# A fused attention and MLP kernel: PSUM banks placed by its planner, head halves of the second token chunk, ReLU over two column blocks, last output in two pieces

## Chip, cores and metric

The kernel runs on one core of a Trainium2 chip. The metric is the device time of one execution in microseconds (us), as the median of several runs. All times below are in us.

## What is computed

There are two stages. The first is attention with a window of 128 tokens and 4 sink tokens; the second is a layer norm and a two-layer MLP with a residual. Batch is 4, heads 8, sequence 768, head size 64, so the model width is 512 and the hidden width 2048.

```python
scores = scale * np.matmul(q, k.transpose(0, 1, 3, 2))
keep = is_sink | in_window            # pos < 4, or 0 <= i - j < 128
a = softmax(np.where(keep, scores, -1e9))
x = np.matmul(a, v)                   # then heads side by side: (4, 768, 512)
xn = (x - mu) / np.sqrt(var + 1e-6) * g_ln
out = x + np.maximum(xn @ w_ch1, 0.0) @ w_ch2
```

Inputs and output are float32; the matrix products run in bfloat16.

## The kernel before

**Tiles.** The 3072 tokens are 24 tiles of 128, six to a batch (tile t is batch t // 6, place r = t % 6). The MLP works on groups of tiles, `GROUPS = [2, 2, 2, 4, 4, 4, 4, 2]`; groups 0 to 2 are batch 0.

**Order.** Nothing is issued in program order. Each piece of work is an `Op` with a cost by engine, a list of ops it needs, the buffers it allocates and uses, and a key. `Plan.emit` (L56) is a list scheduler: it keeps a clock for each engine, finds when each waiting op could start, takes the engine with the earliest start and, among the ops within a small slack of that start, the one with the lowest key; then it emits its instructions. So the order on each engine is fixed at build time by the planner's costs, and on the chip each engine follows it and waits where its inputs are late. Until 26 us of the planned time, `spin` (L194) fills TensorE's planned gaps with matmuls on a constant tile.

**PSUM.** Of the eight banks, four form two wide buffers of two banks (`ps_w`: scores, values, the sinks' v product, batch 1's q/k transposes), one is the bank for transposes of normalized tiles and for the spins (`ps_t`, "bank"), and three are single (`ps_m`: batch 0's q/k transposes, up and down projections, sink scores). Buffers of a pool are handed out in turn.

**Loads.** POOL issues the loads of q, k, v and both weights in one order (`load`, with at most seven in flight in the plan). Batch 0's q and k come in two token chunks of 384: chunk 0 in two halves of four heads for each of q and k, chunk 1 in one piece for q and one for k (L314). The two v tiles of the first rows come before chunk 1. Then come w1 and w2 by quarters (L351, L354) with v tiles between them, and batch 1's q and k as one piece each (L314). Batches 2 and 3 are loaded by tile (L329) and transposed by DMA from SP's queue (`prep`, L411).

**Attention.** Batches 0 and 1 are transposed on TensorE (`prep_runs`, L388) and copied out of PSUM by ACT (L184) or DVE (L186). `scores` (L500) multiplies a tile's keys with 256 queries; for tiles 0 to 3 the mask is added by a matmul (L496). ACT takes the exponential (L511); for other tiles DVE (L515, L521) or POOL (L523, L526) masks it. `sinks` multiplies the four sink keys (L436, L459, L464) and builds the sinks' values (L446, L451). `values` (L560, L567, L570) multiplies with v; DVE then divides (L592, L594), takes statistics (L600, L603) and centers with the gain `gb` (L608). `gb` is spread over the partitions once by a matmul (L737) and copied by ACT or DVE. Tiles below 12 are transposed on TensorE (L647), later ones by DMA from SP (L637).

**MLP.** `up` (L668) makes one 128-column block of the hidden layer for a group: four matmuls of 128 x n tokens, where n is 256 for groups of two tiles and 512 for groups of four. ReLU (L677 on ACT, L679 on DVE) copies it to SBUF. `down` (L699) multiplies a tile with w2 in four quarters of four matmuls with 512 columns, and DVE adds the residual (L712); SP stores the tile (L717).

The few lines of the planner and of `up` that the change rests on:

```python
if len(h) + k >= b.bufs:                      # Plan.emit.ready
    for u in h[k - b.bufs].users:
        if u.end is not None:
            r = max(r, u.end)
...
pb.t = ps_m.tile([128, 512], FP32, name="pm") # up
for j in range(NDM):
    nc.tensor.matmul(pb.t[:, 0:n], lhsT=w1s[:, j, 128 * ht:128 * (ht + 1)], rhs=xtb[g].t[:, j, 0:n], ...)
```

Of the kernel before, what the change touches and what calls it, by code (L numbers as in the profile page):

```python
# [14 lines left out]
class Buf:  # L15


    def __init__(self, pool, bufs):
        self.pool, self.bufs, self.users, self.t = pool, bufs, [], None
# [12 lines left out]
class Plan:  # L32
# [12 lines left out]
    EARLY = 16.0  # L45

# [9 lines left out]
    def emit(self):  # L56
        free, hist = {}, {}
        waiting = list(self.ops)

        def ready(o):  # L60

            r, held = 0.0, False
            for d in o.deps:
                if d.end is None:
                    return None, False

                r = max(r, d.end - (self.LAT[d.eng] + d.lat - 0.03 if len(o.engs) == 1 and d.eng in o.engs else 0.0))
            n = {}
            for b in o.alloc:
                h = hist.get(b.pool, [])  # L70
                k = n[b.pool] = n.get(b.pool, -1) + 1
                if len(h) + k >= b.bufs:
                    for u in h[k - b.bufs].users:
                        if u.end is not None:
                            r = max(r, u.end)
                        elif b.pool == "pw":
                            held = True
                        else:
                            return None, False
            return (None if held else r), held  # L80

        trace = []
        while waiting:
# [22 lines left out]
            if e == "PE" and s < self.WARM:  # L106
                f = max(free.get(e, 0.0), 1.3)
                n = int((min(s, 5.0) - f) / 0.107) if f < 5.0 else 0
                n += int((s - max(f, 5.0) - 0.1) / 0.057) if s > 5.0 else 0
                for _ in range(n if s < 7.0 else 4 * n // 5):  # L110
                    self.spin()
            free[e] = s + c
            o.end, o.eng = s + c + self.LAT[e] + o.lat, e
            for b in o.alloc:
                hist.setdefault(b.pool, []).append(b)
            waiting.remove(o)
# [7 lines left out]
def kernel(  # L124
# [31 lines left out]
    NB0 = 3  # L156
# [18 lines left out]
    ps_w = ctx.enter_context(tc.tile_pool(name="ps_w", bufs=2, space=PS))  # L175
    ps_t = ctx.enter_context(tc.tile_pool(name="ps_t", bufs=1, space=PS))
    ps_m = ctx.enter_context(tc.tile_pool(name="ps_m", bufs=3, space=PS))
# [11 lines left out]
    bank = ps_t.tile([128, 512], FP32, name="bank")  # L189
    pt_view, junk = bank[:, 0:384].bitcast(BF16), bank[:, 384:512]  # L190
    ident = consts.tile([128, 128], BF16)

    def spin():
        nc.tensor.matmul(junk, lhsT=spinner, rhs=spinner, start=True, stop=True, skip_group_check=True)  # L194
# [81 lines left out]
    ident_done = op({"POOL": 0.35}, const_ident, [begun], -499.5)  # L276
    half_masks = op({"POOL": 0.6}, const_masks, [begun], -492)
# [90 lines left out]
    def prep_runs(b, c, hp, key):  # L368
# [5 lines left out]
        kb, pb = kqb[b], Buf("pm", 3) if n > 1 else Buf("pw", 2)  # L374

        def go(_):
            if kb.t is None:
                kb.t = qkt.tile([128, 2, HP, S], BF16, name="qkt")
            if n > 1:
                pb.t = ps_m.tile([128, 512], FP32, name="pm").bitcast(BF16)[:, 0:2 * w]  # L380
            else:
                pb.t = ps_w.tile([128, 2, 512], FP32, name="pw").rearrange("d x m -> d (x m)").bitcast(BF16)
            pb.t = pb.t.rearrange("d (x m) -> d x m", x=2)
            for x in range(2):
                src = qn[(b, x)].t.rearrange("p (c h r d) -> p c h r d", c=n, h=H, r=e)
                for r in range(e):
                    for h2 in range(2):
                        nc.tensor.transpose(pb.t[64 * h2:64 * (h2 + 1), x, 128 * r:128 * (r + 1)],  # L388
                                            src[:, c, 2 * hp + h2, r, :], ident)
# [3 lines left out]
        for xs in ([(0, 1)] if n > 1 else [(0,), (1,)]):  # L393
            def back(eng, x0=xs[0], x1=xs[-1] + 1):
                copy(eng, kb.t[:, x0:x1, hp, c * w:(c + 1) * w].rearrange("d x (p r) -> d x p r", r=e),
                     pb.t[:, x0:x1, 0:w].rearrange("d x (r p) -> d x p r", r=e))

            m = len(xs) * w
            o = op({"DVE": 0.18 + m * 0.00101, "ACT": 0.16 + m * 0.00084}, back, [o0], key, (), [pb, kb])
            for x in xs:  # L400
                prepped[(b, c, hp, x)] = o
# [26 lines left out]
    def sinks(b, key):  # L428
# [3 lines left out]
        pb, eb = Buf("pm", 3), Buf("es", 2)  # L432
# [8 lines left out]
        vb = Buf("pw", 2)  # L441

        def mm_v(_):
            vb.t = ps_w.tile([128, 2, 512], FP32, name="pw")
            for half in range(2):
                nc.tensor.matmul(vb.t[:, half, 0:4 * (D + 1)], lhsT=sel,  # L446
# [3 lines left out]
        def mul_v(_):  # L450
            nc.vector.tensor_tensor(  # L451
                vs.rearrange("p (a h) d -> p a h d", a=2),
                vb.t[:, :, 0:4 * (D + 1)].rearrange("p a (h d) -> p a h d", d=D + 1),
                smask.rearrange("p (a h) -> p a h", a=2).unsqueeze(3).to_broadcast([128, 2, 4, D + 1]), op=ALU.mult)

        def mm(_):
            pb.t = ps_m.tile([128, 512], FP32, name="pm")
# [9 lines left out]
        ov = op({"PE": 0.22}, mm_v, [vcast[(b, 0)], sinks_done, ones_done], key, [vb])  # L467
        vs_done[b] = op({"DVE": 0.7}, mul_v, [ov, vread.get((b - 2, RB - 1))], key, (), [vb])
# [5 lines left out]
    def scores(t, halves, key):  # L474
# [7 lines left out]
        pbs, ebs = [Buf("pw", 2) for _ in parts], [Buf("e", 8) for _ in parts]  # L482
# [6 lines left out]
        def mm(_):  # L489
            for pb, eb, part in zip(pbs, ebs, parts):  # L490
                eb.t = epool.tile([128, 2, 512 // n, n], BF16, name="e")
                pb.t = ps_w.tile([128, 2, 512], FP32, name="pw").rearrange("p a (i c) -> p a i c", c=n)
# [53 lines left out]
    def values(t, key):  # L546
# [3 lines left out]
        pb = Buf("pw", 2)  # L550
# [3 lines left out]
        def mm(_):  # L554
            po = pb.t = ps_w.tile([128, 2, 512], FP32, name="pw")
# [85 lines left out]
        pt = Buf("pt", 1)  # L641

        def tr(_):
            room()
            pt.t = pt_view
# [14 lines left out]
    def up(g, ht, key):  # L660
        n = 128 * GROUPS[g]
        pb = Buf("pm", 3)
        hb = h1b[(g, ht)] = Buf("h1t", NH1 + 6) if n == 512 else Buf("h1n", NB0 * NH1)

        def mm(_):
            pb.t = ps_m.tile([128, 512], FP32, name="pm")
            for j in range(NDM):
                nc.tensor.matmul(pb.t[:, 0:n], lhsT=w1s[:, j, 128 * ht:128 * (ht + 1)], rhs=xtb[g].t[:, j, 0:n],  # L668
                                 start=(j == 0), stop=(j == NDM - 1))

        def act(e):
            if n == 512:
                hb.t = h1pool.tile([128, 512], BF16, name="h1t", bufs=NH1 + 6)
            else:
                hb.t = h1pool.tile([128, 256], BF16, name="h1n", bufs=NB0 * NH1)
            if e == "ACT":
                nc.scalar.activation(hb.t[:, 0:n], pb.t[:, 0:n], AF.Relu)  # L677
            else:
                nc.vector.tensor_scalar_max(hb.t[:, 0:n], pb.t[:, 0:n], 0.0)  # L679

        deps = [turned[FIRST[g] + i] for i in range(GROUPS[g])] + [w_in[(1, ht // 4)]]
        o = op({"PE": 0.865 * n / 512}, mm, deps, key, [pb], [xtb[g]])
        relu[(g, ht)] = op({"ACT": 0.16 + 0.44 * n / 512, "DVE": 0.15 + 0.54 * n / 512}, act, [o], key - 20, [hb], [pb])
# [3 lines left out]
    def down(g, ti, quarter, key):  # L687
        t = FIRST[g] + ti
        alloc = []
        if quarter == 0:  # L690
            pcb[(g, ti)] = Buf("pm", 3)
            alloc = [pcb[(g, ti)]]
        pb = pcb[(g, ti)]

        def mm(_):
            if quarter == 0:
                pb.t = ps_m.tile([128, 512], FP32, name="pm")
            for ht in range(4 * quarter, 4 * quarter + 4):
                nc.tensor.matmul(pb.t, lhsT=h1b[(g, ht)].t[:, 128 * ti:128 * (ti + 1)], rhs=w2s[:, ht, :],  # L699
# [3 lines left out]
        o = op({"PE": 0.865}, mm, [relu[(g, ht)] for ht in hts] + [w_in[(2, max(quarter, 2))], pre_down.get((g, ti))], key,  # L703
               alloc, [pb] + [h1b[(g, ht)] for ht in hts])
        pre_down[(g, ti)] = o
        if quarter == 3:
# [3 lines left out]
            def fin(_):  # L710
                ob.t = opool.tile([128, DM], FP32, name="ot")
                nc.vector.scalar_tensor_tensor(ob.t, in0=pb.t, scalar=rsb[g][:, ti:ti + 1],  # L712
                                               in1=xb[t].t.rearrange("p h d -> p (h d)"),
                                               op0=ALU.mult, op1=ALU.add)

            def put(_):
                nc.sync.dma_start(out[b, 128 * r:128 * (r + 1), :], ob.t)  # L717

            o = op({"DVE": 0.75}, fin, [o, rs_done[g]], key - 20, [ob], [pb, xb[t]])
# [13 lines left out]
    gp = Buf("pm", 3)  # L733

    def spread_g(_):
        gp.t = ps_m.tile([128, 512], FP32, name="pm")
# [3 lines left out]
    gb_done = op({"ACT": 0.6, "DVE": 0.65}, lambda e: copy(e, gb, gp.t), [gb_done], bkey[0] - 1, (), [gp])  # L740

    for half in range(2):
        for x in range(2):
            load_runs(0, 0, x, 4 * half, 4 * half + 4, ((1.5, 1.0), (1.6, 1.1))[half][x], -500 + half)
    for r in range(2):
        load_v(0, r, -491 + r)
    for x in range(2):
        load_runs(0, 1, x, 0, H, (2.8, 2.04)[x], -488 + x)
# [11 lines left out]
    for b in range(B):  # L760
        k0 = bkey[b]
        if b == 0:
            for c in range(2):
                for hp in range(HP):
                    prep_runs(0, c, hp, k0 + (0.6 + 0.1 * hp if c else 0.15 if hp > 1 else -40))
# [31 lines left out]
    for s, g in mlp_order:  # L797
        if s == "u" and g < NB0:
            for ht in range(NH1):
                up(g, ht, 5.2 * (ht // 4) + 1.73 * g + 0.43 * (ht % 4))  # L800
        elif s == "u":
            for ht in range(NH1):
                up(g, ht, up_pos[g] + 0.216 * GROUPS[g] * ht)
        else:
            order = [(ti, qu) for ti in range(GROUPS[g]) for qu in range(4)]
            for n, (ti, qu) in enumerate(order):
                down(g, ti, qu, down_pos[g] + 0.865 * n)
# [38 lines left out]
```

## Time and profile before

| | |
|---|---|
| median of 4 runs | 235.71 (234.17, 234.78, 236.63, 237.29) |
| the profiled execution | 234.17, span 232.5 from first to last instruction |
| mean granted TensorE clock | 0.998 |
| TensorE busy | 221.8 (95%), 1838 matmuls |
| VectorE, ScalarE, GpSimd busy | 114.8, 115.4, 78.4 |
| loaded from and stored to HBM | 27.27 MB, 6.29 MB |

PE is TensorE's matmuls, PEld its weight loads, DVE is VectorE, ACT ScalarE, POOL GpSimd; SP only issues DMAs. A matmul's recorded duration holds the way through the array: neighbours overlap, and what one costs is the distance between two starts. In the timeline and the chain a row gives start, length, engine, line and the tiles written and read, and a bracket gives the idle time before it and what ended it.

### The profile page before, as it was taken

The page shows a single profiled execution, that of the slowest core. Times are in us where ns is not written, and L with a number is a line of the kernel's source. Part 1 is how long each engine was busy: PE and PEld are TensorE (multiplying, and loading weights), DVE is VectorE, ACT ScalarE, POOL GpSimd, SP SyncE. Part 2 cuts the span into 40 slices and gives each one's busy share as a digit, 9 for nine tenths or more (in the row PEclk, how much of TensorE's full clock was granted, in tenths as well). Part 3 has the DMA queues.
Part 4 walks back from the last instruction along what each step waited for, and adds up shares of the span by engine and source line. Part 5 has one row for each costly group of instructions (what it writes and reads, how often), then busy time and mean ns, then how long its engine had stood idle before and what let it go on. Part 6 is the DMA issues. An engine that isn't in the chain of part 4 may idle for free.

```text
span 232.5 us, 4451 instructions
## 1 busy us (share of the span) xinstructions
PE 221.8 (95%) x1838; PEld 124.3 (53%) x1838; DVE 114.8 (49%) x213; ACT 115.4 (50%) x186; POOL 78.4 (34%) x105
## 2 busy tenths in 40 slices
PE   8977999989899999999999999999999999999993
PEld 8643678867455554454555444454444554445851
DVE  1454676066959698755567345662017560022011
ACT  2658787879451625675314873336623156400810
POOL 7985386459121997191201100210005020000000
PEclk9999999999999999999999999999999999999999
DMA  6999999999997999999952202212002221012102
GB/s 69 147 187 193 191 207 204 205 157 155 140 129 183 136 166 179 142 166 142 154 160 68 25 0 71 71 50 62 0 4 81 77 73 20 0 45 93 45 0 90
DMA packets 83478, 24.93 MB, mean 107 GB/s; under 512 B 74241, under 2 KB 80385, under 8 KB 83458
## 3 DMA queue, kind: packets, MB, share of 16 engines
q0 software_dynamic: 60416, 13.64, 68.6%
q1 hardware_dynamic: 23040, 11.02, 24.0%
q8 instruction: 14, 0.23, 0.4%
q14 instruction: 6, 0.05, 0.1%
q10 hardware_dynamic: 2, 0.00, 0.0%
HBM read 27.27 MB, written 6.29 MB: 144 GB/s over the span
## 4 chain that ended last, share of the span: by engine, by line
PE 83%; DVE 7%; DMA 3%; POOL 3%; ACT 2%; issue 1%; POOLq 0%
PE pm L699 36%; PE pm L668 32%; PE pw L500 4%; DMA qkn<-in_k_dram 3%; PE pw L567 2%; PE pw L570 2%; POOL qkn L314 2%; DVE xn L608 1%; PE pw L560 1%; ACT qkt L184 1%; PE bank L647 1%; DVE st L600 1%; DVE xt L594 1%; DVE qkt L186 1%; POOL vn L338 1%; PE pw L388 1%
## 5 line engine op out<-in xcount | busy, mean ns | idle before, releaser
L668 PE MATMUL pm<-xnt,w1s 128*128 128x256 bf16 (+1 forms) x512 | 88.6, 326 | 0.1
L668 PEld LDWEIGHTS <-w1s 128*128 128x128 bf16 x512 | 48.3, 98 | 33.3 <-issue 2.4
L511 ACT ACTIVATE e<-pw 128x1024 bf16<-128x1024 f32 x44 | 43.5, 1021 | 44.2 <-PE pw L500 44.2
L699 PE MATMUL pm<-w2s,h1t 128*128 128x512 bf16 x256 | 57.9, 379 | 0.0
L712 DVE SCALAR_TENSOR_TENSOR ot<-pm,rs,xt 128x512 f32<-128x512 f32 x24 | 18.0, 749 | 61.1 <-PE pm L699 45.8
L677 ACT ACTIVATE h1t<-pm 128x512 bf16<-128x512 f32 x59 | 35.2, 597 | 21.7 <-PE pm L668 21.7
L699 PEld LDWEIGHTS <-h1t 128*128 128x128 bf16 x256 | 24.2, 98 | 28.4 <-issue 0.8
L699 PE MATMUL pm<-w2s,h1n 128*128 128x512 bf16 x128 | 30.0, 379 | 0.0
L677 ACT ACTIVATE h1n<-pm 128x256 bf16<-128x256 f32 x56 | 21.0, 386 | 17.5 <-PE pm L668 15.2
L620 POOL TENSOR_SCALAR ve<-mv 128x2 f32<-128x2 f32 (+1 forms) x8 | 4.8, 601 | 56.4 <-DVE mv L603 56.3
L338 POOL DMA_DIRECT2D vn<-in_v_dram x24 | 21.6, 916 | 0.4 <-DMA qkn<-in_k_dram 0.4
L523 POOL TENSOR_SCALAR_AFFINE_SELECT e<-e 128x512 bf16<-128x512 bf16 (+1 forms) x7 | 4.9, 700 | 44.3 <-ACT e L511 44.3
L608 DVE SCALAR_TENSOR_TENSOR xn<-xt,mv,gb 128x512 bf16<-128x512 bf16 x24 | 18.5, 774 | 2.3 <-DMA xnt<-xn 1.6
L521 DVE TENSOR_TENSOR e<-e,mask 128x1024 bf16<-128x1024 bf16 x23 | 16.3, 710 | 4.9 <-ACT e L511 4.8
L699 PEld LDWEIGHTS <-h1n 128*128 128x128 bf16 x128 | 11.6, 98 | 12.8 <-issue 0.8
L600 DVE BATCH_NORM_STATS2 st<-xt 128x6 f32<-128x512 bf16 x24 | 16.7, 695 | 0.8
L594 DVE TENSOR_TENSOR xt<-pw,rc 128x512 bf16<-128x512 f32 x24 | 16.6, 692 | 0.8
L567 PE MATMUL pw<-vn,e 128*128 128x65 bf16 x192 | 15.8, 193 | 0.0
L567 PEld LDWEIGHTS <-e 128*128 128x128 bf16 x192 | 13.6, 97 | 2.4 <-issue 0.5
L500 PE MATMUL pw<-qkt 64*128 64x256 bf16 (+1 forms) x192 | 14.7, 263 | 0.1
L570 PE MATMUL pw<-vn,e 128*128 128x65 bf16 x160 | 14.2, 193 | 0.0
L500 PEld LDWEIGHTS <-qkt 64*128 64x128 bf16 x192 | 6.7, 94 | 11.2 <-issue 10.5
(62 smaller groups left out, 171.7 us busy)
## 6 DMA issues: line engine op xcount, KB each, us to landing
out_dram<-ot SPq DMA_DIRECT2D x24, 256.0 KB, 2.2
vn<-in_v_dram POOLq DMA_DIRECT2D x24, 128.0 KB, 10.2
w1s<-in_moe_w_ch_dram POOLq DMA_DIRECT2D x4, 512.0 KB, 12.2
w2s<-in_moe_w_ch_dram POOLq DMA_DIRECT2D x4, 512.0 KB, 14.7
qkn<-in_q_dram POOLq DMA_DIRECT2D x12, 128.0 KB, 7.3
qkn<-in_k_dram POOLq DMA_DIRECT2D x12, 128.0 KB, 7.0
qkn<-in_q_dram POOLq DMA_DIRECT2D x1, 768.0 KB, 18.2
qkn<-in_k_dram POOLq DMA_DIRECT2D x1, 768.0 KB, 19.8
```

Of the source, the lines that this page charges most:

```text
L338: nc.gpsimd.dma_start(vn_buf[b % 2][:, r, :, 0:D], v[b, :, 128 * r:128 * (r + 1), :].rearrange("h p d -> p h d"))
L500: nc.tensor.matmul(pb.t[:, h2, i], lhsT=kb.t[64 * h2:64 * (h2 + 1), 1, hp, 128 * r:128 * (r + 1)], rhs=kb.t[64 * h2:64 * (h2 + 1), 0, hp, ...
L511: nc.scalar.activation(eb.t, pb.t, AF.Exp, scale=scale)
L567: nc.tensor.matmul(pv[:, half, hh, :], lhsT=weights_of(t, half, i, h2, 0), rhs=vn[:, r, h, 0:D + 1], start=fresh and hh == 0, stop=(r == 0 ...
L570: nc.tensor.matmul(pv[:, half, hh, :], lhsT=weights_of(t - 1, half, i, h2, 128), rhs=vn[:, r - 1, h, 0:D + 1], start=False, stop=True, ski ...
L594: nc.vector.tensor_tensor(xb[t].t.rearrange("p (a h) d -> p a h d", a=2), pv[:, :, :, 0:D], rc[0].unsqueeze(3).to_broadcast([128, 2, 4, D] ...
L600: nc.vector.bn_stats(st, xf)
L608: nc.vector.scalar_tensor_tensor(xnb[t].t, in0=xf, scalar=mvb[g][:, ti, 0:1], in1=gb, op0=ALU.subtract, op1=ALU.mult)
L668: nc.tensor.matmul(pb.t[:, 0:n], lhsT=w1s[:, j, 128 * ht:128 * (ht + 1)], rhs=xtb[g].t[:, j, 0:n], start=(j == 0), stop=(j == NDM - 1))
L677: nc.scalar.activation(hb.t[:, 0:n], pb.t[:, 0:n], AF.Relu)
L699: nc.tensor.matmul(pb.t, lhsT=h1b[(g, ht)].t[:, 128 * ti:128 * (ti + 1)], rhs=w2s[:, ht, :], start=(ht == 0), stop=(ht == NH1 - 1))
L712: nc.vector.scalar_tensor_tensor(ob.t, in0=pb.t, scalar=rsb[g][:, ti:ti + 1], in1=xb[t].t.rearrange("p h d -> p (h d)"), op0=ALU.mult, op1 ...
```

## The change

1. *Banks.* There is one PSUM pool with fixed buffers: two wide ones (banks 0 to 3) and four single ones (banks 4 to 7). The planner itself picks the buffer that comes free first (`place`, in `emit`); an op may only be planned when the buffer's last user has been planned. The fourth single buffer, the former transposes bank, serves only spins until a planned time of 26 and joins the others then; spins end when it has been taken. Transposes of normalized tiles take a single buffer.
2. *Order in the first 22 us of the plan.* Among ops that start less than 0.5 after the chosen one, and before it would nearly be done, one with a lower key goes first (`HOLD`).
3. *Loads.* Chunk 1 of batch 0's q and k comes in two halves of four heads. The first half is issued before the first two v tiles, the second half after them. The constant for transposes and the masks are made after all four loads of chunk 0.
4. *Copies.* Chunk 0's first two head pairs are copied out of PSUM as q and k apart, instead of both at once; its other two pairs are copied by DVE only. `gb` is copied by DVE only.
5. *Sinks' values.* Batch 0 takes two single buffers for them instead of a wide one; the product on DVE is two instructions instead of one.
6. *ReLU.* For groups of two tiles, `up` fills one bank with two column blocks (eight matmuls) and one ReLU instruction covers both.
7. *Last output.* For the last tile, `down` runs the four quarters for columns 0 to 383, adds the residual and stores them, and then does the same for columns 384 to 511.

```diff
+    HOLD = 22.0, 0.5
...
+        def place(o):
+            r, taken, now = 0.0, [], free.get("PE", 0.0)
+            for b in o.alloc:
+                if b.pool not in ("pw", "pm"):
+                    continue
+                best = None
+                for i in ((0, 2) if b.pool == "pw" else (4, 5, 6) if now < self.WARM else (4, 5, 6, 7)):
+                    v = vacant(i)
+                    if i not in taken and v is not None and (best is None or v < best[0]):
+                        best = v, i
+                if best is None:
+                    return None, b.pool == "pw"
+                r, b.slot = max(r, best[0]), best[1]
+                taken.append(b.slot)
+            return r, False
...
-            if e == "PE" and s < self.WARM:
+            if s < self.HOLD[0]:
+                s, e, o, c = min((x for x in cand if x[1] == e0 and (x[2] is o or x[2].key < o.key - 0.05 and
+                                  x[0] < min(s + c - 0.12, s + self.HOLD[1]))), key=lambda x: (x[2].key, x[0]))
+            if e == "PE" and s < self.WARM and 7 not in tenant:
...
-    ps_w = ctx.enter_context(tc.tile_pool(name="ps_w", bufs=2, space=PS))
-    ps_t = ctx.enter_context(tc.tile_pool(name="ps_t", bufs=1, space=PS))
-    ps_m = ctx.enter_context(tc.tile_pool(name="ps_m", bufs=3, space=PS))
+    psum = ctx.enter_context(tc.tile_pool(name="psum", bufs=1, space=PS))
...
+    wide = [psum.tile([128, 2, 512], FP32, name=f"wide{i}") for i in range(2)]
+    single = [psum.tile([128, 512], FP32, name=f"single{i}") for i in range(4)]
...
-    ident_done = op({"POOL": 0.35}, const_ident, [begun], -499.5)
-    half_masks = op({"POOL": 0.6}, const_masks, [begun], -492)
+    ident_done = op({"POOL": 0.35}, const_ident, [begun], -498.5)
+    half_masks = op({"POOL": 0.6}, const_masks, [begun], -498)
...
-        for xs in ([(0, 1)] if n > 1 else [(0,), (1,)]):
+        for xs in ([(0, 1)] if c or n > 1 and hp > 1 else [(0,), (1,)]):
...
+            if n > 1 and c == 0 and hp > 1:
+                del engs["ACT"]
...
-        vb = Buf("pw", 2)
+        vb = [Buf("pw", 0)] if b else [Buf("pm", 0), Buf("pm", 0)]
...
-    def up(g, ht, key):
+    def up(g, h0, key):
         n = 128 * GROUPS[g]
+        m = 512 // n
...
+            for i in range(m):
+                for j in range(NDM):
+                    nc.tensor.matmul(pb.t[:, n * i:n * (i + 1)], lhsT=w1s[:, j, 128 * (h0 + i):128 * (h0 + i + 1)],
+                                     rhs=xtb[g].t[:, j, 0:n], start=(j == 0), stop=(j == NDM - 1))
...
-                nc.scalar.activation(hb.t[:, 0:n], pb.t[:, 0:n], AF.Relu)
+                nc.scalar.activation(hb.t, pb.t, AF.Relu)
...
-    def down(g, ti, quarter, key):
+    def down(g, ti, quarter, c0, c1, key):
...
-                nc.tensor.matmul(pb.t, lhsT=h1b[(g, ht)].t[:, 128 * ti:128 * (ti + 1)], rhs=w2s[:, ht, :],
+                nc.tensor.matmul(pb.t[:, 0:n], lhsT=hidden(g, ht, ti), rhs=w2s[:, ht, c0:c1],
                                  start=(ht == 0), stop=(ht == NH1 - 1))
...
-            load_runs(0, 0, x, 4 * half, 4 * half + 4, ((1.5, 1.0), (1.6, 1.1))[half][x], -500 + half)
+            load_runs(0, 0, x, 4 * half, 4 * half + 4, ((1.5, 1.0), (1.05, 1.05))[half][x], -500 + half)
+    for x in range(2):
+        load_runs(0, 1, x, 0, HP, 1.2, -496 + x)
     for r in range(2):
         load_v(0, r, -491 + r)
     for x in range(2):
-        load_runs(0, 1, x, 0, H, (2.8, 2.04)[x], -488 + x)
+        load_runs(0, 1, x, HP, H, 1.4, -488 + x)
...
-            order = [(ti, qu) for ti in range(GROUPS[g]) for qu in range(4)]
-            for n, (ti, qu) in enumerate(order):
-                down(g, ti, qu, down_pos[g] + 0.865 * n)
+            at = down_pos[g]
+            for ti in range(GROUPS[g]):
+                for c0, c1 in ((0, 384), (384, DM)) if FIRST[g] + ti == NT - 1 else ((0, DM),):
+                    for qu in range(4):
+                        down(g, ti, qu, c0, c1, at)
+                        at += 0.865 * (c1 - c0) / DM
```

## The prediction

> **What bounds the kernel now.** First the page's engine shares and its 40 slices (5.8 us each), to see which engine is full and where it is not.
>
> ```profile
> PE 221.8 (95%) x1838; PEld 124.3 (53%) x1838; DVE 114.8 (49%) x213; ACT 115.4 (50%) x186; POOL 78.4 (34%) x105
> ...
> PE   8977999989899999999999999999999999999993
> ...
> PEclk9999999999999999999999999999999999999999
> DMA  6999999999997999999952202212002221012102
> ```
>
> TensorE is the only full engine, at full clock. The DMA row is full until slice 19 (116 us): in the first half transfers set when things can start. Next the busy times by stretch, cut where the work changes (columns: length, then busy us and instructions of PE, PEld, DVE, ACT, POOL; clock; DMA share; GB/s).
>
> ```profile
> 6.60:24.10 17.50, 14.69 (x212) 8.11 (x211) 8.28 (x17) 12.30 (x16) 14.18 (x22) 1.00 1.56 180
> 24.10:45.70 21.60, 20.93 (x246) 17.00 (x244) 12.54 (x25) 17.26 (x38) 12.05 (x17) 1.00 1.36 202
> 45.70:61.20 15.50, 13.37 (x208) 10.46 (x208) 10.82 (x20) 12.13 (x23) 10.41 (x12) 1.00 2.36 153
> 61.20:123.00 61.80, 61.80 (x481) 30.97 (x480) 44.46 (x81) 27.82 (x36) 27.16 (x32) 1.00 1.64 153
> 123.00:228.60 105.60, 105.55 (x649) 52.38 (x646) 36.31 (x63) 44.62 (x74) 9.23 (x12) 1.00 0.15 46
> ```
>
> From 61.2 to 228.6 TensorE never waits, and the set of matmuls is the same in both kernels, so that stretch keeps its length. Only three places can change: the start, the stretch 45.7 to 61.2, and the tail after the last matmul. The chain that ended last shows what the second is made of:
>
> ```profile
> 45.76 0.81 PE pw L388 x24
> 46.59 0.81 ACT qkt L184
> 47.42 0.97 DVE qkt L186
> 48.39 0.04 issue
> 48.43 0.88 PE pw L388 x24
> 49.33 0.81 ACT qkt L184
> 50.16 1.83 DVE qkt L186 x2
> ```
>
> These are batch 1's q/k transposes, whose copies out of PSUM release the next ones. They start when batch 1's k has landed. Its issue in the timeline, and its size and time to landing on the page:
>
> ```profile
> 25.56 0.87 POOL L314 DMA_DIRECT2D qkn<-in_k_dram  x1 [1.41 <-DMA w1s<-in_moe_w_ch_dram]
> ```
> ```profile
> qkn<-in_k_dram POOLq DMA_DIRECT2D x1, 768.0 KB, 19.8
> ```
>
> 25.56 + 19.8 = 45.3. The queue in front of it is full (share 1.56 and 1.36 of the stretches, 180 and 202 GB/s) and carries the same bytes in both kernels, so k lands at 45.3 in both; I allow 0.5 us either way.
>
> **Rates.** A matmul row's duration holds its pipeline, so I count starts: 64 of 512 columns in 13.81 us (chain, L699) are 0.216 each; 48 weight loads with 256 columns in 5.18 us (L668) are 0.108 each.
>
> **Step 1, the loads.** Token chunk 1 of q and k goes from two issues to four. Issues cost 0.74 to 0.99 us (L314). Up to w1's first piece POOL then does 3.3 (four issues), 0.9 (identity and masks), 1.55, 1.8 (two v) and 1.55: it is issued at 10.4 instead of 8.95. It landed at 18.5, 9.6 us after issue: the backlog hides the 1.45, and without it the first use (21.7, below) would still be later than 20.0. The identity moves from 3.47 to 4.95; the first transposes wait for data of 6.17. The first v comes after 384 KB more: 10.1 becomes 12.4, hidden since its exponentials end at 13.2. Chunk 1's first half lands near 11 instead of 16.0, so TensorE no longer stands 1.28 us for it (waits: PE pm L388 <- DMA).
>
> **Step 2, the copies for the first scores.** Head pairs 0 and 1 get a q copy on ACT and a k copy on DVE instead of one copy each. In the compiled order each k copy waits for its q copy. Half a copy, from 0.80 and 0.96 (768 elements) and 0.59 on ACT (512), is 0.48 and 0.55: both pairs done at 8.8 instead of 8.46. TensorE is in L737 and two mask matmuls until 8.87, which covers it; uncovered it costs 0.35. Moving the gamma copy to DVE frees 0.58 us of ACT before the first exponential, and DVE has a gap of 2.33 us there.
>
> **Step 3, walking the compiled order to k's landing**, with durations of before. Exponentials of tiles 0 and 1 end at 10.3, 12.1, 13.2, 14.2 (11.4 and 14.7 for the pairs before); values of tile 1 run at 14.4 instead of 16.3; tile 2's exponentials end at 19.6 and 20.6 instead of 21.6 and 24.3. The first up projection starts at 21.7 instead of 24.1. From there TensorE has work in hand: tile 2 and 3 normalized at 27.0 and 29.65 (28.1, 31.4), all of group 0 issued by 31.5, group 1 by 40.5, one down quarter at 40.7 (its last w2 piece of 22.24 + 15.1 = 37.4 is there), two ups of group 2 by 43.4. Then it waits 1.9 us for k: that slack covers errors of the walk.
>
> At that point the compiled orders differ exactly: all other groups equal, L668 has issued 144 narrow matmuls instead of 132, and L699 four instead of none: 12 x 0.108 + 4 x 0.216 = 2.17 us done ahead. It starts at 45.37 instead of 45.69: 0.32. **Gain 2.5.**
>
> The wide ReLU helps that filler: before, 48 narrow ones run before 62 us (40 of 383 ns, 8 of 424), 18.7 us; 24 of about 600 are 14.4. Neither engine is full there, so the 4.3 us count as nothing by themselves. A bank is held for two blocks; the fourth bank pays for that.
>
> **Rule against row.** The Trainium skill, "TensorE: Matmul & The Clock Gate", in the table under "Why this matters for your kernels", says to keep idle gaps under about 3 us, or the clock falls to half. This speaks against a wait with nothing in it, and the spins that fill gaps stop at 26 us. In the row, 1.48 us between starts near 14.6 left the clock at 9s; no longer gap is in the trace. By the row the 1.9 us cost nothing more; by the rule a wait over 3 us costs about 1.7 (half of one 3.4 us window). I take nothing, and keep 1.7 for the range.
>
> **Step 4, from k's landing to the first full down tile.** TensorE's real gaps there before, by starts in the timeline: 0.73 and 0.19 (L388), 0.31 (L500, second score), 0.50 (L446), 1.15 (L647, waiting for xn): 2.9. In the new order two full banks of ups stand behind the first transposes and two behind the second; the copies still go ACT then DVE, so 0.4 and 0.25 stay; the scores then find their copies done at 51.7, and down quarters stand before sink, values and transposes. I leave 0.8. **Gain 2.1.** The work ahead of the first unbroken down run agrees: reached at 59.3 with 2.75 us more done than at 61.15 before.
>
> **Step 5, later.** The first up projection of group 4 (123.0 before) has the same matmuls ahead of it in both orders. It needs tile 13, transposed by DMA between tiles landing at 115.2 and 118.3, about 116.8. TensorE now comes at 118.4. Batch 2's first v (75.9 + 5.2 = 81.1) is needed near 83.3 now. Thin but enough; I charge 0.2. Splitting the sinks' v product adds about 0.1 us of DVE per batch, beside matmuls.
>
> **Step 6, the tail.** The last matmul ends at 228.55; then
>
> ```profile
> 228.59 0.75 DVE ot L712
> ```
> ```profile
> L717 SPq DMA_DIRECT2D out_dram<-ot x1: 332/332/332, 229.4 to 229.4; - x1
> ```
>
> It lands 2.0 later; the span ends 1.1 after that. Now 384 columns are finished and sent while the last 16 matmuls of 128 columns (0.055 each, as the spins at 11.0) run; their result takes 0.15 + 0.15 = 0.30 instead of 0.75: 0.45. The store is a quarter: The Trainium skill, "DMA: Bandwidth & Descriptors", "Anatomy of one DMA — SWDGE (gpsimd) path", puts 2.0 fixed plus bytes by 436 GB/s for POOL's DMAs, so 192 KB less would save 0.45 (estimate); the row here, SP's, has 2.0 in all for 256 KB, so that fixed part does not fit it. No smaller store is in the trace; between 0 and 0.45 I take 0.2. **Gain 0.65.**
>
> **Sum.** 2.5 + 2.1 - 0.2 + 0.65 = 5.05. The profiled execution took 234.17 (span 232.5 and 1.67 around it), so 229.1. It is the fastest of four runs with median 235.71; taken off the median, **230.7**.
>
> **Rivals.**
> - *The banks were not the bound* (0.09). For: PE's wait list shows 6.3 us in all and no free PSUM bank of an up projection among it. Then only the tail and 0.32 are gained: 234.7, no difference that can be told. Against: the 16 matmuls that the compiled order issues earlier are a count, not a wait.
> - *The transfers bind again at group 4* (0.16). Two output stores now stand between batch 2's transposes on SP, about 1.3 us each (SP's spacing), and all that follows on SP and POOL waits. If tile 13 lands 3 later, TensorE waits 3 - 1.6 = 1.4: 232.1. For: DMA full to 116 us. Against: the same stores came before that point anyway.
> - *SP blocks, slower* (0.06). The store of tile 1 stands in front of three of batch 2's transposes. If its result comes late, the chain transposes, v, batch 3's loads, its transposes, tile 13 slips whole. Slack is 1.6, the gain 5, so from 6.6 us it decides; at 10 us the time is 239. Against: that result is due at 64 and SP reaches it near 67.
> - *k lands earlier* (0.10): up to 1.9 us more, 228.8.
>
> The forecast itself has 0.59: 229.2 to 232.2. With the ends of the rivals and the spread of four runs (3.1 us) the range is 228.2 to 234.0. About 1% can be told from no change: faster by more 0.83, within 0.11, slower 0.06.
>
> **What would show it.** Right: first up projection near 21.7; L425's batch 1 transposes still start near 45.4, after a PE wait of 1 to 3 us for qkn; gaps under 1 us in all from there to the downs; TensorE full to about 224; a last result near 0.3. Wrong: a wait of PE for xnt or vn between 75 and 120, a PEclk digit under 9, batch 1's transposes later than 46, or ups that wait for ACT.

## The result, and the profile after

The median of 33 runs of the changed kernel is 233.93 (230.84 to 235.32); 54 runs of the kernel before have 235.41. The ratio is **0.9895, with a 95% interval of 0.9873 to 0.9918**: about 2.5 us faster, where the sum had 5.05. This ratio leaves out runs over 1.5% above their kernel's fastest, 15 of the 33 and one of the 54, so that the changed kernel looks better by it than by the medians over all runs, which give 1.5 us.

The trace after is of an execution of 234.66 (span 233.0), the trace before of one of 234.17 (span 232.5).

The page after, the rows that answer to those of before (busy time and share; 40 slices of 5.8 us):

```profile
PE 222.1 (95%) x1841; PEld 124.9 (54%) x1841; DVE 116.6 (50%) x217; ACT 108.6 (47%) x155; POOL 84.3 (36%) x111
...
PE   8999999999999999999759999999999999999994
...
PEclk9999999999999999999979999999999999999999
DMA  6999999999997799999962101312001321012102
```

Counted from 0, TensorE's slices 2 to 11 (12 to 70 us) are full now. A hole is new: 7 and 5 in slices 19 and 20, with a 7 in the clock's row at slice 20. The busy times by stretch (columns as before: length; PE, PEld, DVE, ACT, POOL; clock; DMA share; GB/s) put times on it:

```profile
6.60:24.10 17.50, 16.27 (x217) 8.78 (x217) 10.68 (x21) 12.14 (x16) 15.94 (x24) 1.00 1.59 185
24.10:45.90 21.80, 21.18 (x254) 17.32 (x251) 13.33 (x25) 13.55 (x22) 12.69 (x15) 1.00 1.35 202
45.90:59.40 13.50, 13.23 (x176) 9.39 (x177) 8.13 (x14) 10.20 (x14) 10.98 (x13) 1.00 2.39 151
59.40:114.60 55.20, 55.20 (x447) 28.06 (x445) 39.24 (x73) 27.08 (x36) 30.04 (x36) 1.00 1.71 151
114.60:119.40 4.80, 0.29 (x5) 0.14 (x4) 2.21 (x4) 0.00 (x0) 0.00 (x0) 0.94 1.01 160
119.40:123.00 3.60, 3.60 (x32) 1.79 (x31) 3.35 (x7) 0.30 (x1) 0.00 (x0) 0.60 0.51 170
```

Up to 59.4 the kernel gets about as far as was forecast. In the 4.8 us from 114.6 TensorE has five instructions, and in the 3.6 us after that it runs at 0.60 of its clock. The chain that ended last shows the first part, batch 1's q/k transposes:

```profile
25.62 20.28 DMA qkn<-in_k_dram
45.89 0.04 issue
45.94 0.55 PE wide L425 x12
...
47.33 0.97 DVE qkt L219
48.30 0.04 issue
48.34 0.86 PE wide L425 x24
49.21 0.00 issue
49.21 0.86 PE wide L425 x24
50.07 1.85 PE single L715 x16
```

The first copies still go ACT, then DVE. After the second 48 transposes the chain stays on TensorE, with 16 up matmuls, where before it went through copies on ACT and DVE again. How far ahead TensorE is can be read at the values of tile 16. The first row is from TensorE's timeline before, the other two from the timeline after:

```profile
119.13 0.27 PE L560 MATMUL pw<-vs,es 128*128 128x260 bf16 x1
```
```profile
114.48 0.27 PE L604 MATMUL wide<-vs,es 128*128 128x260 bf16 x1
119.26 0.23 PE L611 MATMUL wide<-vn,e 128*128 128x65 bf16 x1 [4.50 <-DVE e L565]
```

It comes to these values 4.65 us earlier and then stands for 4.50: the second matmul of the tile is at 119.26, where before it was at 119.24. All that had been won is given back in one place. The bracket names a mask on VectorE; why that was late is in VectorE's timeline, before and then after:

```profile
113.47 0.18 DVE L603 BATCH_NORM_AGGREGATE mv<-st 128x2 f32<-128x6 f32 x1
115.21 0.90 DVE L608 SCALAR_TENSOR_TENSOR xn<-xt,mv,gb 128x512 bf16<-128x512 bf16 x1 [1.55 <-DMA xnt<-xn]
```
```profile
108.89 0.18 DVE L647 BATCH_NORM_AGGREGATE mv<-st 128x2 f32<-128x6 f32 x1
117.19 0.75 DVE L652 SCALAR_TENSOR_TENSOR xn<-xt,mv,gb 128x512 bf16<-128x512 bf16 x1 [8.12 <-DMA xnt<-xn]
117.86 0.75 DVE L768 SCALAR_TENSOR_TENSOR ot<-single,rs,xt 128x512 f32<-128x512 f32 x1
118.53 1.28 DVE L565 TENSOR_TENSOR e<-e,mask 128x1024 bf16<-128x1024 bf16 x2
```

Centering tile 15 writes into one of the three buffers for normalized tiles (xn), the one that tile 12 had. That buffer is free when tile 12's DMA transpose has read it. The masks of tile 16 (L565) stand behind the centering in VectorE's order, and TensorE behind the masks. SP's timeline, before and after, shows when tile 12's transpose is issued:

```profile
95.44 12.13 SPq L411 DMA_TRANSPOSE qkt<-qkn  x7
107.66 4.38 SPq L637 DMA_TRANSPOSE xnt<-xn  x3
```
```profile
95.38 12.49 SPq L451 DMA_TRANSPOSE qkt<-qkn  x8
107.96 5.14 SPq L681 DMA_TRANSPOSE xnt<-xn  x3
```

It stands behind batch 3's q/k transposes (the rows show those from 95.4 on) and is issued at 107.7 and 108.0. It landed at 115.1 before and at 117.1 after. So the compute came 4.65 earlier to a release that had not come earlier, and in this execution came 2.0 later. The wait of 1.55 that was in the trace of before, harmless there, became 8.12: 1.55, about 4.6 of lead and 2.0.

Then the clock. From the values of tile 16 to the next scores took 1.56 before (119.24 to 120.80) and 2.92 after (119.26 to 122.18): 1.36 more. The granted clock was half from 118.85 to 122.27. The tail gives 0.8 back: from the last matmul's end to the span's end 3.1 (229.86 to 232.96) instead of 3.9 (228.55 to 232.46):

```profile
229.06 0.62 DVE L768 SCALAR_TENSOR_TENSOR ot<-single,rs,xt 128x384 f32<-128x384 f32 x1 [1.85 <-PE single L755]
229.71 0.96 SPq L773 DMA_DIRECT2D out_dram<-ot  x2
229.96 0.35 DVE L768 SCALAR_TENSOR_TENSOR ot<-single,rs,xt 128x128 f32<-128x128 f32 x1 [0.28 <-PE single L755]
```

So this one execution was even with before at 119.2, lost 1.36, gained 0.07 more up to the last matmul (229.86 against 228.55) and 0.8 in the tail, and ended at 233.0 against 232.5.

### The profile page after: what moved, and what is told of

Same layout as the page of the kernel before. It is cut to its first block, busy times and chain, and to the rows that moved or that the text cites. A ratio compares the mean times of both kernels' runs of the same rounds, so it can differ in the third digit from the quotient of the medians.

```text
span 233.0 us, 4467 instructions
## 1 busy us (share of the span) xinstructions
PE 222.1 (95%) x1841; PEld 124.9 (54%) x1841; DVE 116.6 (50%) x217; ACT 108.6 (47%) x155; POOL 84.3 (36%) x111
## 4 chain that ended last, share of the span: by engine, by line
PE 73%; DMA 17%; POOL 5%; DVE 2%; SPq 1%; issue 1%; ACT 0%; POOLq 0%; DVEq 0%
PE single L755 33%; PE single L715 29%; DMA qkn<-in_k_dram 9%; DMA w1s<-in_moe_w_ch_dram 5%; PE wide L544 4%; DMA xnt<-xn 3%; POOL qkn L351 3%; PE wide L611 2%; PE wide L614 2%; POOL vn L375 1%; PE wide L604 1%; PE wide L425 1%; SPq L681 1%; POOL w1s L388 1%; PE single L691 1%
## 5 line engine op out<-in xcount | busy, mean ns | idle before, releaser
L715 PE MATMUL single<-xnt,w1s 128*128 128x256 bf16 (+1 forms) x512 | 88.2, 326 | 0.0
L555 ACT ACTIVATE e<-wide 128x1024 bf16<-128x1024 f32 x44 | 43.5, 1022 | 49.0 <-PE wide L544 49.0
L755 PE MATMUL single<-w2s,h1t 128*128 128x512 bf16 x256 | 58.8, 383 | 0.0
L768 DVE SCALAR_TENSOR_TENSOR ot<-single,rs,xt 128x512 f32<-128x512 f32 (+2 forms) x25 | 18.2, 728 | 58.6 <-PE single L755 43.4
L724 ACT ACTIVATE h1t<-single 128x512 bf16<-128x512 f32 x60 | 35.9, 598 | 21.8 <-PE single L715 21.6
L755 PE MATMUL single<-w2s,h1n 128*128 128x512 bf16 (+2 forms) x144 | 30.3, 356 | 0.0
L724 ACT ACTIVATE h1n<-single 128x512 bf16<-128x512 f32 x29 | 17.2, 597 | 24.3 <-PE single L715 24.1
L611 PE MATMUL wide<-vn,e 128*128 128x65 bf16 x192 | 16.2, 196 | 4.5 <-DVE e L565 4.5
L565 DVE TENSOR_TENSOR e<-e,mask 128x1024 bf16<-128x1024 bf16 x21 | 15.2, 731 | 6.1 <-ACT e L555 6.1
L638 DVE TENSOR_TENSOR xt<-wide,rc 128x512 bf16<-128x512 f32 x24 | 16.6, 692 | 0.8
L544 PE MATMUL wide<-qkt 64*128 64x256 bf16 (+1 forms) x192 | 14.7, 264 | 0.0
L614 PE MATMUL wide<-vn,e 128*128 128x65 bf16 x160 | 14.6, 196 | 0.0
```

Of the source, the lines that this page charges most:

```text
L544: nc.tensor.matmul(pb.t[:, h2, i], lhsT=kb.t[64 * h2:64 * (h2 + 1), 1, hp, 128 * r:128 * (r + 1)], rhs=kb.t[64 * h2:64 * (h2 + 1), 0, hp, ...
L555: nc.scalar.activation(eb.t, pb.t, AF.Exp, scale=scale)
L611: nc.tensor.matmul(pv[:, half, hh, :], lhsT=weights_of(t, half, i, h2, 0), rhs=vn[:, r, h, 0:D + 1], start=fresh and hh == 0, stop=(r == 0 ...
L614: nc.tensor.matmul(pv[:, half, hh, :], lhsT=weights_of(t - 1, half, i, h2, 128), rhs=vn[:, r - 1, h, 0:D + 1], start=False, stop=True, ski ...
L638: nc.vector.tensor_tensor(xb[t].t.rearrange("p (a h) d -> p a h d", a=2), pv[:, :, :, 0:D], rc[0].unsqueeze(3).to_broadcast([128, 2, 4, D] ...
L715: nc.tensor.matmul(pb.t[:, n * i:n * (i + 1)], lhsT=w1s[:, j, 128 * (h0 + i):128 * (h0 + i + 1)], rhs=xtb[g].t[:, j, 0:n], start=(j == 0), ...
```

## The experiments

The theory is that the wait for the buffer, and the slow clock after it, ate the forecast gain. Its rivals: the early stretch brought less than it seemed, or the slack went elsewhere. Ratios are against runs of the kernel before on the same chip (medians 234.14 to 234.81).

**More buffers.** The extra room is made by a narrower padding of v (`VD`); the instructions and their order are those of the changed kernel.

```diff
-    VD = 96
+    VD = 80
-    xnpool = ctx.enter_context(tc.tile_pool(name="xnpool", bufs=3))
+    xnpool = ctx.enter_context(tc.tile_pool(name="xnpool", bufs=6))
```

> The changed kernel with six buffers for the normalized tiles instead of three (the v buffers' padding goes from 96 to 80 to make room); the order of instructions on every engine is that of the changed kernel. Theory A (tile 15's centering waits on DVE for tile 12's DMA transpose, the mask behind it holds TensorE 4.5 us, and the clock falls after that wait): the gap before values at 114.6 goes, no PEclk digit under 9, 4.5 + 1.4 us less than the changed kernel's profile, so about 229 in a fast run and a ratio to before of 0.973 to 0.978. Rival B (the wait only moves on, to the first up projection of group 4, which needs tile 13's DMA transpose): a new PE wait near 118 of 3 us or more, under 2 us gained, ratio 0.983 or more. Rival C (the first 60 us gave less than 4.5): ratio about 0.985 with no PE wait anywhere.

Measured: median 228.17, ratio **0.9745 (0.9704 to 0.9786)**, span 226.3. VectorE's timeline has the same centering with no bracket:

```profile
108.33 0.18 DVE L647 BATCH_NORM_AGGREGATE mv<-st 128x2 f32<-128x6 f32 x1
108.55 0.75 DVE L652 SCALAR_TENSOR_TENSOR xn<-xt,mv,gb 128x512 bf16<-128x512 bf16 x1
```

TensorE has no wait at tile 16, its mean clock is 1.000, and its last matmul ends at 223.26. The result is about 6.0 us under before (0.0255 of 234.2), 3.5 under the changed kernel.

**The padding alone**, as a control: only the `VD` line.

> The changed kernel with the v buffers padded to 80 instead of 96 values a head and nothing else: the control for the first run. Every theory: the changed kernel's own time, ratio to before 0.987 to 0.992, with the wait of 4 to 5 us at 114.6 still there. If the padding itself matters, the v loads land earlier or later than 8.4 us after issue and the ratio moves.

Measured: median 231.84, ratio 0.9873 (0.9827 to 0.9919), not to be told from the changed kernel's. The padding isn't the cause. Its trace has the same hole, smaller in this execution, and the clock after it (timeline, then the stretch of 3.4 us):

```profile
114.06 0.27 PE L604 MATMUL wide<-vs,es 128*128 128x260 bf16 x1
116.11 0.20 PE L611 MATMUL wide<-vn,e 128*128 128x65 bf16 x1 [1.78 <-DVE e L565]
```
```profile
117.10:120.50 3.40, 3.07 (x17) 1.08 (x14) 2.69 (x7) 1.02 (x1) 0.00 (x0) 0.50 0.43 154
```

The same wait is 1.8 us here and 4.5 in the changed kernel, with the same instruction order: it depends on when tile 12's transpose lands, at 113.95 here and at 117.1 there. That one wait differs by so much between executions would widen the spread of the changed kernel's runs. The spread alone doesn't show it: it is 4.5 us in 33 runs, but 4.3 in the 54 of the kernel before.

**Spins in the hole**, to take the clock's part by itself: 80 matmuls on the constant tile, into the bank that the values are about to overwrite.

```diff
             po = pb.t = room_for(pb)
+            for _ in range(80 if t == 16 else 0):
+                nc.tensor.matmul(po[:, 0, 0:128], lhsT=spinner, rhs=spinner, start=True, stop=True, skip_group_check=True)
```

> The changed kernel with 80 spin matmuls (0.055 each, 4.4 us) in front of tile 16's values, into a bank that these values then overwrite: TensorE works while it waits for DVE. Theory A: the wait for the mask still ends at about 119, but the clock stays at 9 in the slices after it, and 1.0 to 1.5 us are gained on the changed kernel (ratio 0.983 to 0.985). Rival (the fallen clock is a disturbance that has nothing to do with the wait): no gain, ratio 0.989, or a PEclk digit under 9 at the same place.

Measured: median 232.91, ratio 0.9935 (0.9912 to 0.9957): above the changed kernel's ratio, where a gain was expected (by the medians of all runs the two are alike, 0.9945 and 0.9937). The clock did stay full (TensorE's timeline with the spins, VectorE's with the masks, then the stretch):

```profile
114.34 4.63 PE L601 MATMUL wide<-spinner 128*128 128x128 bf16 x80
118.81 0.27 PE L606 MATMUL wide<-vs,es 128*128 128x260 bf16 x1
```
```profile
115.92 1.28 DVE L565 TENSOR_TENSOR e<-e,mask 128x1024 bf16<-128x1024 bf16 x2
```
```profile
117.10:120.50 3.40, 3.34 (x57) 2.71 (x57) 1.52 (x4) 0.00 (x0) 0.00 (x0) 1.00 0.52 176
```

But the spins are of fixed length and the wait is not. In the changed kernel TensorE went on 0.73 after the two masks began (118.53 to 119.26); here they began at 115.92, so it could have gone on at about 116.65 (an estimate from these rows), and it was in spins until 118.8. The overstay of some 2.2 is more than the 1.36 that the slow clock cost in the changed kernel's trace.

The mean clock of every run is on record and says how often the clock fell. A window of 3.4 us at half clock takes 0.5 x 3.4 / 233 = 0.007 off the mean. Of the 48 runs of the kernel before beside these experiments, 36 have 0.996 or more and 12 have 0.990 to 0.993; where most of them were run, in the 26 beside this run, their medians are 234.1 and 235.8, 1.7 apart. Of the changed kernel's 33 runs three have 0.998 or more (median 231.1), 19 about 0.992 (233.4), and 11 about 0.985 (234.8), as two such windows would give; no trace shows where a second one lies. With spins all 13 have 0.999 or more. So the clock fell in nearly every run of the changed kernel, and in a quarter of those of before. Its share of the loss is not separated: a longer wait and a fallen clock come together.

**Six buffers in the kernel before**: the same two lines.

> The kernel before with six buffers for the normalized tiles (padding 80). Theory A: DVE's wait of 1.6 us for the DMA transpose goes, but no PE wait hung on it, so the time is that of before (ratio 0.998 to 1.002). Rival (the three buffers bound before as well): faster by 1 us or more, ratio 0.995 or less, which would make the buffers and not the change the lever.

Measured: median 234.44, ratio 1.001 (0.9984 to 1.0036). Before, the 1.55 us wait for the buffer held nothing that mattered; the lever exists only when compute is earlier. The change's own worth, both sides with six buffers, is thus about 6.2 us (1.001 - 0.9745, of 234.2).

**One part undone at a time, with six buffers**, so that the later wait doesn't hide the part's worth. First the fourth single bank, which never joins the others:

```diff
-                for i in ((0, 2) if b.pool == "pw" else (4, 5, 6) if now < self.WARM else (4, 5, 6, 7)):
+                for i in ((0, 2) if b.pool == "pw" else (4, 5, 6)):
```

> The first run's kernel (changed, six buffers for normalized tiles) but the fourth single bank never joins: three for projections and transposes together. Theory (the fourth bank is what lets TensorE run ahead in the first 60 us): 1 to 2 us slower than the first run, ratio to before 0.979 to 0.983, with PE waits on ACT or DVE behind L715. Rival (the banks are not the bound): the compiled order still has 144 narrow ups and four downs ahead of batch 1's transposes, so within 0.4 us of the first run, ratio 0.973 to 0.976.

Measured: median 229.58, ratio 0.9791 (0.9763 to 0.9819); against six buffers with all parts (0.9745) that is 1.1 us, which the two intervals don't tell from nothing. Three waits of TensorE are in its list that six buffers alone don't have or have shorter. The third is a single bank not yet read by ReLU; the second is a load, and e2_pad80 and e9_xn4, with all four banks, have it too (0.8 and 1.9):

```profile
PE single L691 <- DVE xn L652: 0.8, 2, 0.6
PE single L425 <- DMA qkn<-in_q_dram: 0.8, 1, 0.8
PE single L715 <- ACT h1t L724: 0.7, 1, 0.7
```

Then ReLU over one block (`up` with one block per bank, costs and buffers scaled to it):

```diff
-        m = 512 // n
+        m = 1
...
-                nc.scalar.activation(hb.t, pb.t, AF.Relu)
+                nc.scalar.activation(hb.t[:, 0:n], pb.t[:, 0:n], AF.Relu)
```

> The first run's kernel with ReLU over one column block of 256 again (one block to a bank). The order has 144 ups but no down ahead of batch 1's transposes (0.86 less). Theory (wide ReLU by itself is beside the matmuls): 0.3 to 1.0 us slower than the first run, ratio 0.976 to 0.979. Rival (the 4.3 us of ACT and DVE that it saves were on the path): 2 us or more slower, ratio 0.983 or more, with gaps before L715 that end on ACT.

Measured: median 230.14, ratio 0.9818 (0.9792 to 0.9844): 1.7 us, the largest of the four and the only one whose interval lies clear of that of six buffers (up to 0.9786). It lies between what was expected and the rival's figure, and the rival's gaps before up matmuls that end on ACT aren't in the list. Ahead of batch 1's transposes it has issued 144 up matmuls of 256 columns and no down, instead of 144 and four (0.86 less). In the stretch from 45.9 to 59.4 us TensorE is busy for 12.69, with six buffers alone for 13.21. Two rows of its wait list:

```profile
PE wide L425 <- DMA qkn<-in_k_dram: 0.8, 1, 0.8
PE wide L425 <- DVE qkt L219: 0.7, 1, 0.7
```

The copy on VectorE between the transposes holds TensorE 0.7 instead of 0.2, and the work in front of k's landing is shorter. That this is due to ReLU instructions standing in the way, and not to the planner's other order, isn't separated.

Then chunk 1 in one piece each for q and k, after the first two v tiles:

```diff
-    for x in range(2):
-        load_runs(0, 1, x, 0, HP, 1.2, -496 + x)
...
-        load_runs(0, 1, x, HP, H, 1.4, -488 + x)
+        load_runs(0, 1, x, 0, H, (2.8, 2.04)[x], -488 + x)
```

> The first run's kernel with chunk 1 of batch 0's q and k in one piece each, after the first two v tiles. Theory (the head halves bring the first up projection forward by about 2 us, but TensorE is held again at batch 1's k near 45): first up back near 23.5, batch 1's transposes start within 1 us of the first run's 45.0, 0.3 to 1.5 us slower in all, ratio 0.976 to 0.981. Rival (the halves are the whole gain of the first 45 us): 2.5 us slower, ratio 0.985.

Measured: median 229.10, ratio 0.9775 (0.9747 to 0.9804): 0.7 us, which the two intervals don't tell from nothing. The wait is back, 1.8 us for k (`PE single L425`, 1.1 the longest) instead of 0.7, but the first up projection starts at 22.25, not later than with the halves (22.75 in the changed kernel, 22.89 with six buffers, 24.13 in e9_xn4 below). These traces don't show that the halves bring that one forward.

Last, the last output in one piece:

```diff
-                for c0, c1 in ((0, 384), (384, DM)) if FIRST[g] + ti == NT - 1 else ((0, DM),):
+                for c0, c1 in ((0, DM),):
```

> The first run's kernel with the last output in one piece. Theory: the tail after the last matmul goes from 3.0 back to 3.95, 0.8 to 1.0 us slower, ratio 0.978 to 0.979. Rival (the store's time does not depend on its size): 0.4 slower, ratio 0.976.

Measured: median 229.55, ratio 0.9791 (0.9763 to 0.9818): 1.1 us, not told from nothing by the intervals either; but the trace shows the tail itself: the last matmul ends at 223.35 and the span at 227.28, 3.9 as before the change.

**Four buffers instead of six.** Is one more buffer enough, or does the wait move to tile 16? The edit against the changed kernel, with the same `VD` as above:

```diff
-    xnpool = ctx.enter_context(tc.tile_pool(name="xnpool", bufs=3))
+    xnpool = ctx.enter_context(tc.tile_pool(name="xnpool", bufs=4))
```

> After with four buffers for xn instead of six (same padding of v as in e1_xn6, same instruction order). Tile 15 then takes the buffer of tile 11, whose transpose had landed long before 108, so the wait of VectorE for it at 109 should be gone; tile 16 takes tile 12's, free at about 117. Theory (one buffer's lateness is all that cost the time): tile 16's centering comes only after its values, at 116.75 with six buffers, so VectorE waits at most 1 us there, with TensorE in matmuls beside it; TensorE has no wait over 0.5 us at 114 to 118, the clock row stays at 9, the last matmul ends near 223.5, and the ratio is 0.972 to 0.979 as with six. Rival (the wait only moves one tile on): VectorE waits about 3 us or more at tile 16, the masks or evictions behind it hold TensorE 1 us or more near 118 to 120, and the ratio stands between 0.980 and 0.988.

Measured: median 228.46, ratio **0.9724 (0.969 to 0.9758)**, the same as six. Tile 15's centering is at 109.76 and tile 16's, which takes tile 12's buffer, at 117.96, neither with a wait:

```profile
117.74 0.18 DVE L647 BATCH_NORM_AGGREGATE mv<-st 128x2 f32<-128x6 f32 x1
117.96 0.75 DVE L652 SCALAR_TENSOR_TENSOR xn<-xt,mv,gb 128x512 bf16<-128x512 bf16 x1
```

One more buffer recovers as much as three more. What the expectation says of tile 11 is off in one detail: tiles below 12 are transposed on TensorE, so no DMA holds that buffer.

## Why the prediction was right on the start and missed the middle

The forecast was 230.7, in a range of 228.2 to 234.0. The median of 233.93 lies in that range by 0.07 and outside the forecast's own band (229.2 to 232.2). The gain is 1.5 by the medians and 2.5 by the ratio, instead of 5.05. That the range still holds it is owed to its width, not to the mechanism: the loss came from a place that the text doesn't name. One of its signs of being wrong, a PEclk digit under 9, did show.

**Steps 1 to 3** held in kind. w1's first piece is issued at 10.10 (10.4 forecast), k lands at 45.89 (45.3), 144 ups of 256 columns and four downs stand ahead. The walk was too fast: the first up projection starts at 22.75, not 21.7, and TensorE comes to batch 1's transposes at 44.93, not 43.4. It does twelve and then waits 0.48 instead of 1.9:

```profile
44.93 0.53 PE L425 MATMUL wide<-ident,qkn 128*64 128x128 bf16 x12
45.94 1.20 PE L425 MATMUL wide<-ident,qkn 128*64 128x128 bf16 x36 [0.48 <-DMA qkn<-in_k_dram]
```

That slack absorbed the walk's error, as it was meant to. In e1_xn6 and e9_xn4 it is used up: there the transposes start at 45.03 and 46.24 and run without a wait. The first 48 are over at 47.06 where before it was 47.15, so the part is worth 2.16 (the count; 2.17 in the text) and 0.09: 2.25 instead of 2.5.

**Step 4** made good for it: at tile 16's values the lead is 4.65, where Steps 3 and 4 had 2.5 + 2.1 = 4.6. Step 4's share is then 2.4, and two small errors cancel. That the 4.3 us less of ReLU time "count as nothing by themselves" is not confirmed: e6_relu1 shows 1.7 us for the wide form as a whole, twice the 0.86 of the four downs that it brings forward. What the rest is isn't separated.

**Step 5 is the one that failed.** It charged 0.2 for what comes after the first 60 us; the runs show about 3.5 (0.9895 against 0.9745 with six buffers). It followed the DMA transposes only to their reader on TensorE, tile 13 at group 4's first up projection, and found a slack of 1.6 there. It didn't follow them to what they release on VectorE. The wait list of VectorE before held the row all along:

```profile
DVE xn L608 <- DMA xnt<-xn: 1.6, 1, 1.6
```

A wait of 1.6 us for a DMA that stays where it is becomes 1.6 + 4.65 = 6.25 when the compute in front of it comes 4.65 earlier. Measured were 8.1, where the landing was 2.0 later than before, and 5.4 (e2_pad80) and 5.7 (e3_spin), where it was 1.2 and 0.6 earlier. Behind it stand the mask and then TensorE, which waited 4.5 in the first and 1.8 in the second. The rival "the transfers bind again at group 4" had the cause, transfers that don't move with the compute, and its 232.1 is near the median of the ratio (0.9895 of 235.41 is 232.9), but named another place, the first up projection of group 4, and TensorE has no wait there. Its "all that follows on SP and POOL waits" is in the traces in part: batch 3's first load is issued 1.6 later than before (POOL's timeline, before and after).

```profile
81.19 0.94 POOL L329 DMA_DIRECT2D qkn<-in_q_dram  x1
```
```profile
82.78 0.94 POOL L366 DMA_DIRECT2D qkn<-in_q_dram  x1
```

**Rule against row** went against the reading taken from the row. The Trainium skill, "TensorE: Matmul & The Clock Gate", in the table under "Why this matters for your kernels", wants gaps below about 3 us; that agrees with the changed kernel, where 4.5 us of gap were followed by half a clock for 3.42 us (118.85 to 122.27) at a cost of 1.36. But e2_pad80 has the same length of slow clock (117.07 to 120.48) after TensorE stood only 1.78 us, while in e9_xn4 it stood 1.92 near 12 us with the clock full (1.00 from 10 to 20 us):

```profile
12.46 0.36 PE L425 MATMUL single<-ident,qkn 128*64 128x128 bf16 x6 [1.92 <-DMA qkn<-in_q_dram]
```

So the length of one gap doesn't decide alone, and 3 us was no safe limit here. The 1.9 us wait that Step 3 had counted as free could have cost what the text kept for its range; that price, 1.7, is also the difference between the medians of the runs of the kernel before with and without a fallen clock.

**Step 6** was under-sized: 0.8 in the changed kernel and with six buffers (tails of 3.10 and 3.07 instead of 3.91), against 0.65. VectorE's last row is 0.35 instead of 0.75: 0.40 (0.45 forecast). The store of 128 columns landed 1.58 after its issue and that of 384 columns 1.89, against 2.01 for a whole tile: 0.43 where 0.2 was taken. The upper end, from the Trainium skill, "DMA: Bandwidth & Descriptors", "Anatomy of one DMA — SWDGE (gpsimd) path", was the better one: its price for the bytes, given for POOL's DMAs, agrees with these stores of SP (0.45 for 192 KB less, an estimate, against 0.43), its fixed 2.0 doesn't, since 1.58 is the whole of the smallest.

**The sum.** With the buffer out of the way the time is 6.0 us under before by the ratio, where the sum without Step 5's charge was 5.25. The terms had about the right size in total (the interval of that ratio is 1 us to a side); the missing one was about 3.5 us with the other sign.

**Still open.** The four parts undone singly come to 1.1 + 1.7 + 0.7 + 1.1 = 4.6 of 6.2; the rest lies with the planner's early order, the copies and the sinks' values, or with how they combine, and wasn't tried apart. Each interval is about 0.003 to 0.004 wide to a side, so each part is known to some 1 us only.

Why tile 12's transpose landed 3.1 us later in the changed kernel's trace (117.1) than in e2_pad80's (113.95) is shown in part. Of this, 1.9 is there when batch 3's twelve q/k transposes begin (SP's timeline, changed kernel and e2_pad80), before which SP waited 5.1 and 3.6 for a q load; why that came later isn't shown.

```profile
89.56 18.31 SPq L451 DMA_TRANSPOSE qkt<-qkn  x12
```
```profile
87.63 18.23 SPq L451 DMA_TRANSPOSE qkt<-qkn  x12
```

## What to carry to other kernels

When a change brings compute forward, go through every engine's waits for DMA and add the gain to each, harmless ones too: a transfer that is queued behind others need not move with the compute, and a buffer that it frees can become the next bound. Follow a release to all who wait for it, the buffer's next writer as well as the data's reader, and to what stands behind that writer on its engine. If a first stretch works as forecast and the total doesn't, compare the start of the same work in both timelines until the lead vanishes; the row there names the cause.

## What was not expected of the hardware

- The clock was halved for 3.41 us after TensorE had stood 1.78 us (e2_pad80), and not after it had stood 1.92 (e9_xn4).
- With one and the same instruction order, TensorE's wait at one place was 1.8 us in one trace and 4.5 in another: the DMA transpose behind it was issued 2.0 later in the second (105.95 and 107.96) and took 9.1 us to land instead of 8.0.
- The kernel before, too, has a mean clock of 0.990 to 0.993 in 12 of 48 runs, and takes about 1.7 us more in them.
- SP's stores took 2.01 us for 256 KB, 1.89 for 192 KB and 1.58 for 64 KB: most of it doesn't depend on the size.
